# LSH attention and MoE on one core: scores in float16 pairs for all batches, fixed scales with a check at the end, and another order of batch 0

## The chip, the cores and the metric

The kernel runs on one core of a Trainium2 chip. The metric is the device time of one execution in microseconds (us). A core has a matrix engine (TensorE: PE, its weight loads PEld), three engines for elementwise work (VectorE: DVE, ScalarE: ACT, GpSimd: POOL) and a queue that issues transfers (SyncE: SP). Matrix results land in PSUM, eight banks of 512 float32 numbers in each of 128 partitions; everything else lives in SBUF.

## The reference

There are 4 batches of 8 heads with 768 positions of 64 numbers. A query sees only the keys that fall in the same of 64 buckets, which the signs of six projections give. The attention's output goes through two dense layers with a squared ReLU between them.

```python
q_bits = (np.einsum('bhsd,dk->bhsk', q, proj) > 0)      # 6 bits: a bucket
k_bits = (np.einsum('bhsd,dk->bhsk', k, proj) > 0)
mask = q_bucket[:, :, :, None] == k_bucket[:, :, None, :]
scores = np.where(mask, 0.125 * np.matmul(q, k^T), -1e9)
scores = scores - scores.max(axis=-1, keepdims=True)
attn = np.exp(scores); attn = attn / (attn.sum(-1, keepdims=True) + 1e-9)
x = (attn @ v) as (3072 tokens, 512)                   # 8 heads of 64 side by side
h = np.maximum(x @ w_in, 0.0)                          # 512 x 2048
out = h * h @ w_out                                    # 2048 x 512
```

q, k and v are float32 with a spread of 0.1; the two weight matrices are float64.

## The kernel before

**Precision.** An operand of a matrix product is split in two float16 numbers (high and low part), and three products are summed: high by high, high by low, low by high. `move` writes the high part and `left` the rest. So that float16 holds them, values and weights are first scaled by a power of two that the kernel finds from the data: `split` squares each fetched tile of a weight, sums over the partitions with a matmul against ones (`pt`), takes the largest (`norm`) and makes the factor in `scales`; `scale_values` does the same for v from a Square with a running sum (`sqv`). `fetch` turns float64 into float32 with a shift and an OR. Because each group of four w_out tiles gets its own scale, the first MoE stage adds its output up in four parts (`acc`), and `align` then multiplies all of w_out (`wo<-wo,rel`) so that later stages need not.

**Scores.** `prep` makes the operands of a pair of heads. R holds the transposed keys above the transposed queries. For batches 1 to 3 the two parts are kept in a 32-bit reduced float (A the high, L the low part; the profile prints it as f32), five transfers in SBUF rearrange them in Q, A, M and L, and a unit of scores is two products of 128 rows for each half of the keys: q high and low by k high, then q high by k low together with a mask code that pulls unequal buckets far below. The code comes from the bits through a matmul `pc` and a DVE operation that writes M. For batch 0 (`plain`) there is one product in full float32 with M above and the keys and queries beside it, with fewer transfers.

**Units and visits.** A unit is 128 queries of one head: scores into `pS`, the row maximum on DVE (`nmx`), the exponential on ACT (`e`, its sum in `sm`), then the reciprocal `rv`. Then the weights are normalised and split (`hl`: ACT the high part, DVE the low one) and a transfer transposes them into `aT`. In the visits of PLAIN_AV (numbers 0, 2 and 4) a unit instead divides on POOL, transposes six blocks with TensorE (`pT`) and copies them out of PSUM to a float32 `aT`. There are 192 units in 32 visits; a visit is one half of the queries (3 units) of a pair of heads. After the six units `av` makes the product with the values (`pA`) and splits it (`xx`). `pS` has one place of two banks; while u < 36, odd units use the banks of `po` instead.

**MoE stages.** When all four pairs of one half of a batch are done, `moe` adds a stage: 16 steps of 12 matmuls `pm` (384 columns) and 9 matmuls `po` (512 columns), with ReLU, square and split between them on ACT and DVE. There are eight stages of 112 paced groups each. WHOLE = {0: 2} makes batch 0 go through both halves of its first two pairs and only then to the first halves of the others, so that its first half is whole after six visits, 36 units.

**Order.** All operations are first recorded; `Program.order` then simulates the five queues with costs and ranks, and `emit` writes each queue's instructions in that order. PACE holds the m-th group of MoE matmuls back until a given unit has begun: group 0 at unit 25, 120 at unit 64, 640 at unit 193; the last 256 groups have no unit to wait for. Where the simulated TensorE would sit idle ahead of the first MoE work, `emit` puts matmuls on `ones` (`idle`). One line, 410, records nearly all instructions, so the profile tells groups apart by tiles.

Of the kernel before, what the change touches and what calls it, by code (L numbers as in the profile page):

```python
# [36 lines left out]
BUFS = dict(xx=12, hl=3, raw=2, f=7, e=3, aT=3, g=2, A=2, Q=2, L=2, M=2, RV=2, VV=6)  # L37
# [20 lines left out]
PACE = ((25, 0), (64, 120), (193, 640))  # L58
# [58 lines left out]
class Program:  # L117
# [11 lines left out]
    def tile(self, pool, kind, shape, dtype, name, bufs=1, tag=None):  # L129
# [291 lines left out]

@with_exitstack
def lsh_attention_moe(ctx: ExitStack, tc, kq, v, proj2, w_in, w_out, consts, out):
# [10 lines left out]
    def send(out, x):  # L434
        sp.dma_start(out, x)
# [32 lines left out]
    sgn_f = sb([P, 4 * P], F32, "sgn_f", tag="o")  # L468
# [6 lines left out]
    dve.tensor_copy(sgn, sgn_f)  # L475
# [21 lines left out]
    def fetch(src):  # L497

        raw = sb([P, 512, 2], U32, "raw", BUFS["raw"])
# [3 lines left out]
        move(first[:, :, 1], raw.rearrange("p n t -> p (n t)").bitcast(BF16).rearrange("p (n t) -> p n t", t=4)[:, :, 2], 1.0, (dve, pool))  # L503
# [63 lines left out]
    f32 = lambda x: x.bitcast(F32)  # L567
# [74 lines left out]
    def values(b, hp, plain):  # L642
# [14 lines left out]
    def unit(st, half, i, aT, plain):  # L657
        c0 = half * HS + i * P
        u = pr.rank
        pS = ps([P, 3, 512], F32, "pS2", tag="po") if u % 2 and u < ALTERNATE else ps([P, 2, 512], F32, "pS")  # L660
# [6 lines left out]
        nmx = sb([P, 1], F32, "nmx", 2)  # L667
# [211 lines left out]
```

## Time and profile before

| | us |
|---|---|
| three runs | 910.83, 911.90, 917.73 |
| median | 911.90 |
| span of the profiled execution, first to last instruction | 911.7 |
| TensorE's mean granted clock in it | 0.990 |

The record does not say which of the three runs was profiled; its span is 0.2 us under the median. The busy time of TensorE in the profile overlaps for successive matmuls, so its 96% is no measure of how much of the time it had work to issue. For that, one reads the distance between the starts of successive matmuls in the timeline.

| stretch of the span, us | what runs in it |
|---|---|
| 0 to 95 | units 0 to 23, first weights |
| 95 to 253 | units 24 to 63; the first MoE matmul at 153.5 |
| 253 to 745 | units 64 to 190, MoE between them |
| 745 to 911.7 | the rest of the MoE stages, one more unit |

### The profile page before, as it was taken

Reading aid. Unit: us, or ns where it says so; the run is one execution under the profiler, and the core shown is the slowest. Engines: PE = TensorE matmul, PEld = TensorE weight load, DVE = VectorE, ACT = ScalarE, POOL = GpSimd, SP = SyncE. Lnnn points to the kernel's source line nnn. Section 1 sums busy time; section 2 is a strip of 40 time slices with the busy share of each in tenths; the row PEclk is TensorE's granted clock in tenths of the full one; section 3 lists DMA queues with packets and bytes.
Section 4 is the critical chain, followed back from the end, with each engine's and each line's share of the span. In section 5 each row is a group of like instructions: output and inputs, shape, how many; then the busy total and the mean of one; then the engine's idle time right before and its main releaser. Section 6 shows DMA issues by size and latency. Waiting matters only on the chain. (4 is left out here: it accounts for less than half of the span.)

```text
span 911.7 us, 14110 instructions
## 1 busy us (share of the span) xinstructions
PE 871.3 (96%) x5038; PEld 472.1 (52%) x5038; DVE 614.6 (67%) x1150; ACT 664.4 (73%) x1208; POOL 75.7 (8%) x120
## 2 busy tenths in 40 slices
PE   7977987999989999999999999999999999999997
PEld 5543533455545555555555555555555555544553
DVE  4999898989796777787677767885867651211111
ACT  4989797989798777896787777886768663542433
POOL 0433222201000000000000000000000000000000
PEclk9999999999999999999999999999999999999999
DMA  7788778997979897979698979896969561200000
GB/s 234 194 200 185 192 178 192 226 204 166 194 169 203 160 197 139 221 167 203 127 219 157 192 115 196 171 190 126 199 123 194 96 100 28 60 1 1 35 1 36
DMA packets 298790, 136.54 MB, mean 150 GB/s; under 512 B 277088, under 2 KB 277216, under 8 KB 298720
## 3 DMA queue, kind: packets, MB, share of 16 engines
q1 hardware_dynamic: 298720, 135.64, 71.5%
q8 instruction: 40, 0.66, 0.3%
q14 instruction: 30, 0.25, 0.1%
HBM read 37.30 MB, written 6.29 MB: 48 GB/s over the span
## 5 line engine op out<-in xcount | busy, mean ns | idle before, releaser
L410 PE MATMUL po<-wo,g 128*128 128x512 f16 x1152 | 335.3, 380 | 2.4 <-ACT acc L410 0.8
L410 PE MATMUL pm<-xx,win 128*128 128x384 f16 x1536 | 323.8, 326 | 1.0 <-ACT g L410 0.7
L410 DVE TENSOR_REDUCE nmx<-pS 128x1 f32<-128x768 f32 x192 | 182.9, 953 | 63.3 <-PE pS L410 62.4
L410 ACT ACTIVATE e<-pS,nmx 128x768 f32<-128x768 f32 x192 | 172.5, 899 | 61.1 <-DVE nmx L410 56.4
L410 PEld LDWEIGHTS <-win 128*128 128x128 f16 x1536 | 145.7, 98 | 116.1 <-issue 18.1
L410 DVE SCALAR_TENSOR_TENSOR hl<-e,rv,hl 128x768 f16<-128x768 f32 x174 | 176.3, 1015 | 27.8 <-ACT hl L410 27.0
L410 ACT ACTIVATE hl<-e,rv 128x768 f16<-128x768 f32 x174 | 161.7, 931 | 23.8 <-ACT e L410 16.7
L410 PEld LDWEIGHTS <-g 128*128 128x128 f16 x1152 | 107.5, 98 | 131.4 <-issue 28.0
L410 DVE SCALAR_TENSOR_TENSOR g<-g,g 128x384 f16<-128x384 f32 x125 | 69.2, 554 | 134.1 <-ACT g L410 133.1
L410 ACT ACTIVATE g<-pm 128x384 f32<-128x384 f32 x128 | 62.4, 487 | 108.1 <-PE pm L410 106.0
L410 ACT ACTIVATE g<-g 128x384 f32<-128x384 f32 (+1 forms) x252 | 131.2, 521 | 6.8 <-PE po L410 1.8
L407 PE MATMUL pA<-aT,VV 128*64 128x384 f16 x1044 | 110.0, 333 | 0.0
L410 PE MATMUL pS<-A,Q 128*128 128x384 f32 x288 | 93.2, 404 | 2.8 <-ACT e L410 2.8
L407 PEld LDWEIGHTS <-VV 128*64 128x64 f16 x1044 | 53.9, 109 | 54.0 <-issue 37.2
L410 POOL TENSOR_SCALAR rv<-sm 128x1 f32<-128x1 f32 x77 | 37.3, 485 | 511.2 <-ACT e L410 477.6
L410 PE MATMUL pS<-L,M 128*128 128x384 f32 x288 | 77.2, 348 | 1.8 <-DMA M<-Q 1.8
L410 PEld LDWEIGHTS pS<-A,Q 128*128 128x128 f32 x288 | 47.1, 189 | 31.6 <-ACT e L410 22.0
L410 PEld LDWEIGHTS pS<-L,M 128*128 128x128 f32 x288 | 51.9, 188 | 5.8 <-issue 3.9
L410 PE MATMUL pS<-A,L 128*128 128x384 f32 x96 | 41.0, 553 | 9.8 <-ACT L L410 4.9
L410 PE MATMUL pS<-Q,M 128*128 128x384 f32 x96 | 38.2, 516 | 7.8 <-ACT e L410 7.7
L410 DVE TENSOR_SCALAR M<-pc,cst 128x384 fp32r<-128x384 f32 (+1 forms) x56 | 37.6, 671 | 3.9 <-PE pc L410 3.9
L410 ACT ACTIVATION_READ_ACCUMULATOR e<-pS,nmx 128x1 f32 x192 | 38.1, 198 | 0.0
(93 smaller groups left out, 586.3 us busy)
## 6 DMA issues: line engine op xcount, KB each, us to landing
R<-kq SPq DMA_DIRECT2D x24, 384.0 KB
raw<-w_in SPq DMA_DIRECT2D x16, 511.8 KB
raw<-w_out SPq DMA_DIRECT2D x16, 511.8 KB
V<-vp SPq DMA_DIRECT2D x16, 384.0 KB
out<-o SPq DMA_DIRECT2D x21, 256.0 KB
Q<-L SPq DMA_DIRECT2D x24, 192.0 KB
Q<-A SPq DMA_DIRECT2D x24, 192.0 KB
L<-M SPq DMA_DIRECT2D x24, 192.0 KB
```

The costliest lines, as they stand in the source:

```text
L407: ins = q.engine.matmul(*map(real, args), **kw).ins
L410: ins = getattr(q.engine, o.name)(*map(real, o.args), **{k: real(x) for k, x in o.kw.items()}).ins
```

## The change

The kernel becomes two programs. The first (`fast`) runs with fixed scales and fills a flag; behind it each engine loads the flag into a register, and a branch runs the second, general program if the flag is 1. The general one is the kernel before without its special treatment of batch 0. In the fast program:

- Scores are float16 pairs in all batches: `balance` scales keys by 1/4 and queries by 1/2, `prep` always makes A, L, Q and M (now float16, eight places each, so that all four pairs of batch 0 are kept), and the mask code fits float16 with `masks`. The full-float32 product of batch 0 is gone.
- Weights are scaled by 256 for nothing in `fetch` (its factor becomes 2.0) and values by 16; `split` has no squares, sums and factors, `scale_values`, `align` and the four-part sum of the first stage go, and every stage's result is scaled by a constant.
- PLAIN_AV has visits 0 to 5. WHOLE = {0: 0}: batch 0 takes the first halves of its four pairs first, so that a half is whole after four visits, 24 units; then the second halves in reverse. `pS` alternates while u < 24; from there `pT` uses the bank `misc`. PACE lets MoE groups begin at unit 19 and has 140 and 660 where there were 120 and 640.
- `verify` loads q, k and v once more (48 loads of 128 x 768 numbers into the places of `e`), squares q and k on ACT, takes the largest of v and of the weights on DVE, sums squares of w_in with 16 matmuls, looks at every unit's maximum and sum, and writes the flag. The ninth step of the last MoE stage waits for that.

```diff
-BUFS = dict(xx=12, hl=3, raw=2, f=7, e=3, aT=3, g=2, A=2, Q=2, L=2, M=2, RV=2, VV=6)
+BUFS = {
+    True: dict(xx=12, hl=3, raw=2, f=3, e=3, aT=3, g=2, A=8, Q=8, L=8, M=8, R=2, VV=4),
+    False: dict(xx=12, hl=3, raw=2, f=7, e=3, aT=3, g=2, A=2, Q=2, L=2, M=2, R=2, VV=6),
+}
...
-PLAIN, ALTERNATE = 4, 36
-
-PLAIN_AV, DIVIDE = (0, 2, 4), ("pool",)
-
-WHOLE = {0: 2}
-
+ALTERNATE = {True: 24, False: 0}
+
+PLAIN_AV, DIVIDE = (0, 1, 2, 3, 4, 5), ("pool",)
+
+WHOLE = {0: 0}
 
 WIN_AT, WOUT_AT = (0, 2), 1
 FIRST = len(WIN_AT)
 
-PACE = ((25, 0), (64, 120), (193, 640))
+PACE = ((19, 0), (64, 140), (193, 660))
+
+CHECK_RANK = 200
+
+
+QS, KS = 2.0**-1, 2.0**-2
+VS, WS = 2.0**4, 2.0**8
+HS2 = 2.0**-9
+QK_MAX, V_MAX, V_MIN, W_MAX, W_MIN, NORM_MAX = 16.0, 1.0, 2.0**-4, 2.0**15, 2.0, (1.38 * WS) ** 2
...
+def lsh_attention_moe(tc, kq, v, proj2, w_in, w_out, consts, out):
+    with tc.tile_pool(name="fl", bufs=1) as pool:
+        flag = pool.tile([1, 1], mybir.dt.int32, name="flag")
+        run(tc, kq, v, proj2, w_in, w_out, consts, out, flag)
+        general = tc.nc.values_load(flag[0:1, 0:1], min_val=0, max_val=1)
+        with tc.If(general > 0):
+            run(tc, kq, v, proj2, w_in, w_out, consts, out, None)
+
+
 @with_exitstack
-def lsh_attention_moe(ctx: ExitStack, tc, kq, v, proj2, w_in, w_out, consts, out):
+def run(ctx: ExitStack, tc, kq, v, proj2, w_in, w_out, consts, out, flag):
+    fast = flag is not None
+    bufs_of = BUFS[fast]
...
+    masks = cst
+    if fast:
+        parts = lambda x: x.rearrange("p (n t d) -> p n t d", t=2, d=D)
+        dve.tensor_scalar(parts(sgn)[:, :, 0], parts(sgn_f)[:, :, 0], 2.0 / BIG, 2.0**15, ALU.mult, ALU.mult)
+        dve.tensor_scalar(parts(sgn)[:, :, 1], parts(sgn_f)[:, :, 1], 2.0, 2.0**14, ALU.mult, ALU.mult)
+        masks = sb([P, 2], F32, "masks")
+        dve.memset(masks[T, 0:1], 3 * 2.0**16)
+        dve.memset(masks[T, 1:2], -65504.0)
+        dve.memset(masks[U, 0:1], 2.0**16)
+        dve.memset(masks[U, 1:2], 0.0)
+        balance = sb([P, 1], F32, "balance")
+        dve.memset(balance[T], KS)
+        dve.memset(balance[U], QS)
+        maxes, sums = sb([P, UNITS], F32, "maxes"), sb([P, UNITS], F32, "sums")
+    else:
+        dve.tensor_copy(sgn, sgn_f)
+        balance = cst[:, 2:3]
...
-        move(first[:, :, 1], raw.rearrange("p n t -> p (n t)").bitcast(BF16).rearrange("p (n t) -> p n t", t=4)[:, :, 2], 1.0, (dve, pool))
+        move(first[:, :, 1], raw.rearrange("p n t -> p (n t)").bitcast(BF16).rearrange("p (n t) -> p n t", t=4)[:, :, 2], 2.0 if fast else 1.0, (dve, pool))
...
+        if fast:
+            for f, (hi, lo) in zip(fs, parts):
+                move(hi, f)
+                left(lo, f, 1.0, hi)
+            return 1.0, 1.0
...
-    def prep(b, hp, plain):
+    def prep(b, hp):
         r0 = pr.rank
-        Rs, Rqs = [], []
+        Rs = []
         for odd in range(2):
-            R = sb([P, S], F32, "Q" if odd else "A") if plain else sb([P, S], F32, "R", 2)
+            R = sb([P, S], F32, "R")
             send(R, kq[b, 2 * hp + odd])
             Rs.append(R)
-            if plain:
-                Rq = sb([P, S], F32, "R", 2)[T]
-                send(Rq, kq[b, 2 * hp + odd, U])
-                Rqs.append(Rq)
 
         pd = ps([P, 512], F32, "pd", tag="misc")[:, 0:HS]
         matmuls(*[(pd[32 * n : 32 * n + 32], pj, Rs[n // 2][:, n % 2 * HS : (n % 2 + 1) * HS]) for n in range(4)])
@@ -588,33 +633,22 @@
         out = []
         for odd, R in enumerate(Rs):
             pr.rank = r0
-            if plain:
-                M = sb([P, S], F32, "M" if odd else "L")
-            else:
-
-                A, L, Q, M = [sb([P, S], F32R, name) for name in "ALQM"]
-                move(A, R, cst[:, 2:3])
-                left(L, R, cst[:, 2:3], f32(A))
+            A, L, Q, M = [sb([P, S], F16 if fast else F32R, name) for name in "ALQM"]
+            move(A, R, balance)
+            left(L, R, balance, f32(A))
             pr.rank = r0 + STACKS
-            if not plain:
-                send(f32(Q[T]), f32(A[U]))
-                send(f32(Q[U]), f32(L[U]))
-                send(f32(A[U]), f32(A[T]))
+            send(f32(Q[T]), f32(A[U]))
+            send(f32(Q[U]), f32(L[U]))
+            send(f32(A[U]), f32(A[T]))
             for half in range(2):
                 w = slice(half * HS, (half + 1) * HS)
                 n = 2 * odd + half
                 pc = ps([P, 512], F32, "pc", tag="misc")[:, 0:HS]
                 pe.matmul(pc, sgn[:, n * P : (n + 1) * P], bits, start=True, stop=True)
-                dve.tensor_scalar(M[:, w], pc, cst[:, 0:1], cst[:, 1:2], ALU.subtract, ALU.max)
-            if plain:
-
-                move(R[U], M[T], 1.0, MV)
-                move(M[T], Rqs[odd], SC)
-                out.append(((M, R),))
-            else:
-                send(f32(L[U]), f32(M[T]))
-                send(f32(M[T]), f32(Q[T]))
-                out.append(((Q, A), (M, L)))
+                dve.tensor_scalar(M[:, w], pc, masks[:, 0:1], masks[:, 1:2], ALU.subtract, ALU.max)
+            send(f32(L[U]), f32(M[T]))
+            send(f32(M[T]), f32(Q[T]))
+            out.append(((Q, A), (M, L)))
...
-        if b not in vscales:
-            scale_values(b)
-        if plain:
-            return loaded[b, hp]
-        RV = loaded.pop((b, hp))
+        if fast:
+            vscales[b] = VS, None
+            RV = sb([P, 2, KC, D], F32, "V", tag="VV" if plain else "R")
+            send(RV, v[b, hp])
+            if plain:
+                return RV
+        else:
+            if b not in vscales:
+                scale_values(b)
+            RV = loaded.pop((b, hp))
...
-        pS = ps([P, 3, 512], F32, "pS2", tag="po") if u % 2 and u < ALTERNATE else ps([P, 2, 512], F32, "pS")
+        pS = ps([P, 3, 512], F32, "pS2", tag="po") if u % 2 and u < ALTERNATE[fast] else ps([P, 2, 512], F32, "pS")
...
-        nmx = sb([P, 1], F32, "nmx", 2)
+        nmx = maxes[:, u : u + 1] if fast else sb([P, 1], F32, "nmx", 2)
-        sm = sb([P, 1], F32, "sm", 2)
+        sm = sums[:, u : u + 1] if fast else sb([P, 1], F32, "sm", 2)
...
-                pT = ps([P, 512], F32, "pT", tag=("pm", "pA")[g])[:, 0:HS]
+                pT = ps([P, 512], F32, "pT", tag=("pm", "pA")[g] if u < ALTERNATE[fast] else "misc")[:, 0:HS]
...
+        if fast:
+            return 1.0 / (WS * 64)
...
+        grouped = n == 0 and not fast
+        if not grouped:
             pr.rank = RANK_MOE
             back = unscaled(b)
         for f in range(NF + 1):
+            if f == NF // 2:
+                pr.checked = len(pr.ops)
...
+    def verify():
+        pr.rank = CHECK_RANK
+        grade = sb([P, 64], F32, "grade")
+        good = sb([P, 4, 64], F32, "good", tag="hl")
+        dve.memset(good, 1.0)
+        bound = lambda to, x, value, op: dve.tensor_scalar(to, x, value, 1.0, op, ALU.mult)
+        for n in range(2 * B * H // 2):
+            X = sb([P, S], F32, "X", tag="e")
+            send(X, kq[n // H, n % H])
+            pr.add((act, "activation", (X, X, AF.Square), {"scale": 0.25, "accum_out": grade[:, n : n + 1]}))
+        for n in range(B * H // 2):
+            X = sb([P, S], F32, "X", tag="e")
+            send(X, v[n // (H // 2), n % (H // 2)].rearrange("p t c d -> p (t c d)"))
+            dve.tensor_reduce(grade[:, 32 + n : 33 + n], X, AX.X, ALU.max, apply_absolute_value=True)
+        for n in range(NCC):
+            dve.tensor_reduce(grade[:, 48 + n : 49 + n], win[:, 0, n], AX.X, ALU.max, apply_absolute_value=True)
+            dve.tensor_reduce(grade[:, 52 + n : 53 + n], wo[:, 0, 4 * n : 4 * n + 4], AX.XY, ALU.max, apply_absolute_value=True)
+            pt = ps([P, 512], F32, "pt", tag="misc")
+            for cc in range(NCC):
+                sq = sb([P, 512], BF16, "sq", tag="raw")
+                square(sq, win[:, 0, cc, n * 512 : (n + 1) * 512])
+                pe.matmul(pt, ones, sq, start=cc == 0, stop=cc == NCC - 1)
+            dve.tensor_reduce(grade[:, 56 + n : 57 + n], pt, AX.X, ALU.max)
+        dve.memset(grade[:, 60:64], 1.0)
+        bound(good[:, 0, 0:32], grade[:, 0:32], QK_MAX, ALU.is_le)
+        bound(good[:, 0, 32:48], grade[:, 32:48], V_MAX, ALU.is_le)
+        bound(good[:, 1, 32:48], grade[:, 32:48], V_MIN, ALU.is_ge)
+        bound(good[:, 0, 48:56], grade[:, 48:56], W_MAX, ALU.is_le)
+        bound(good[:, 1, 48:56], grade[:, 48:56], W_MIN, ALU.is_ge)
+        bound(good[:, 0, 56:60], grade[:, 56:60], NORM_MAX, ALU.is_le)
+        bound(maxes, maxes, 2.0**30, ALU.is_lt)
+        bound(sums, sums, float(S), ALU.is_equal)
+        dve.tensor_tensor(sums, sums, maxes, ALU.max)
+        worst = sb([P, 2], F32, "worst")
+        dve.tensor_reduce(worst[:, 0:1], good.rearrange("p a b -> p (a b)"), AX.X, ALU.min)
+        dve.tensor_reduce(worst[:, 1:2], sums, AX.X, ALU.min)
+        both = sb([P, 1], BF16, "both")
+        dve.tensor_tensor(both, worst[:, 0:1], worst[:, 1:2], ALU.min)
+        pt = ps([P, 512], F32, "pt", tag="misc")[:, 0:1]
+        pe.matmul(pt, ones, both, start=True, stop=True)
+        bad = pr.given(flag, "flag")
+        dve.tensor_scalar(bad, pt[0:1], P - 0.5, 1.0, ALU.is_lt, ALU.mult)
+        pr.ops[pr.checked].deps.add(len(pr.ops) - 1)
...
-        sts, aTs, plain = kept[b, hp], [], n in PLAIN_AV
+        sts, aTs, plain = kept[b, hp], [], fast and n in PLAIN_AV
...
+    if fast:
+        verify()
```

More of the change, by code (lines that the diff above doesn't have):

```diff
@@ L27 @@
 HS = 384
+UNITS = B * H * S // P
 KC = S // P
@@ L136, in tile, with given @@
         return View(rec, self.shadow.dram_tensor(f"{name}_{self.n}", shape, dtype, kind="Internal").ap(), ())
+    def given(self, real, name):
+        rec = Buffer("sb", int(np.prod(real.shape[1:])), None, lambda: real)
+        return View(rec, self.shadow.dram_tensor(name, real.shape, real.dtype, kind="Internal").ap(), ())
     @staticmethod
@@ L451, in sb @@
     def sb(shape, dtype, name, bufs=1, tag=None):
-        return pr.tile(sbp, "sb", shape, dtype, name, BUFS.get(tag or name, bufs), tag)
+        return pr.tile(sbp, "sb", shape, dtype, name, bufs_of.get(tag or name, bufs), tag)
     def ps(shape, dtype, name, bufs=1, tag=None):
@@ L467, in lsh_attention_moe @@
     sp.dma_start(pj[:, NB : 2 * NB], proj2[:, 3 * NB : 4 * NB])
-    sgn_f = sb([P, 4 * P], F32, "sgn_f", tag="o")
+    sgn_f = sb([P, 4 * P], F32, "sgn_f", tag="raw" if fast else "o")
     dve.memset(sgn_f, 0.0)
@@ L474, in lsh_attention_moe @@
     sgn = sb([P, 4 * P], BF16, "sgn")
-    dve.tensor_copy(sgn, sgn_f)
+    masks = cst
[15 more added lines that the diff above has]
+        balance = cst[:, 2:3]
     thr = sb([P, 1], F32, "thr")
@@ L497, in fetch @@
     def fetch(src):
-        raw = sb([P, 512, 2], U32, "raw", BUFS["raw"])
+        raw = sb([P, 512, 2], U32, "raw", bufs_of["raw"])
         send(raw.rearrange("p n t -> p (n t)").bitcast(U16)[:, 0:2047], src.bitcast(U16)[:, 1:2048])
@@ L547, in split_wout @@
         back = split([w_out[:, n] for n in range(4 * j, 4 * j + 4)], [(wo[:, 0, n], wo[:, 1, n]) for n in range(4 * j, 4 * j + 4)], "wo")[1]
+        if fast:
+            return
         z = zs[:, j : j + 1]
@@ L564, in align @@
             move(x, x, rel[:, n // 4 : n // 4 + 1])
-    f32 = lambda x: x.bitcast(F32)
+    f32 = lambda x: x if fast else x.bitcast(F32)
     def matmuls(*args, start=True, stop=True):
         pr.add((pe, "matmuls", [(a, {"start": start, "stop": stop}) for a in args], {}))
-    def prep(b, hp, plain):
+    def prep(b, hp):
         r0 = pr.rank
-        Rs, Rqs = [], []
+        Rs = []
         for odd in range(2):
-            R = sb([P, S], F32, "Q" if odd else "A") if plain else sb([P, S], F32, "R", 2)
+            R = sb([P, S], F32, "R")
             send(R, kq[b, 2 * hp + odd])
             Rs.append(R)
-            if plain:
-                Rq = sb([P, S], F32, "R", 2)[T]
-                send(Rq, kq[b, 2 * hp + odd, U])
-                Rqs.append(Rq)
         pd = ps([P, 512], F32, "pd", tag="misc")[:, 0:HS]
@@ L666, in unit @@
         sS = pS[:, 0:2, 0:HS]
-        nmx = sb([P, 1], F32, "nmx", 2)
+        nmx = maxes[:, u : u + 1] if fast else sb([P, 1], F32, "nmx", 2)
         dve.tensor_reduce(nmx, sS, AX.XY, ALU.max, negate=True)
-        e = sb([P, S], F32, "e", BUFS["e"])
-        sm = sb([P, 1], F32, "sm", 2)
+        e = sb([P, S], F32, "e", bufs_of["e"])
+        sm = sums[:, u : u + 1] if fast else sb([P, 1], F32, "sm", 2)
         act.activation(e.rearrange("p (j s) -> p j s", j=2), sS, AF.Exp, bias=nmx, accum_out=sm)
@@ L685, in unit @@
             return
-        hl = sb([P, 2, S], F16, "hl", BUFS["hl"])
+        hl = sb([P, 2, S], F16, "hl", bufs_of["hl"])
         move(hl[:, 0], e, rv)
@@ L716, in moe @@
         po, gs = None, {}
-        if n:
+        grouped = n == 0 and not fast
+        if not grouped:
             pr.rank = RANK_MOE
@@ L734, in moe @@
                 g32 = sb([P, HS], F32, "g32", 2)
-                pr.add((act, "activation", (g32, pm[:, 0:HS], AF.Relu), {"scale": 2.0**-23}),
-                       (dve, "tensor_scalar", (g32, pm[:, 0:HS], 2.0**-23, 0.0, ALU.mult, ALU.max), {}))
+                pr.add((act, "activation", (g32, pm[:, 0:HS], AF.Relu), {"scale": HS2 if fast else 2.0**-23}),
+                       (dve, "tensor_scalar", (g32, pm[:, 0:HS], HS2 if fast else 2.0**-23, 0.0, ALU.mult, ALU.max), {}))
                 square(g32, g32)
@@ L745, in moe @@
                 pr.mark = None
-                first, last = (m % 4 == 0, m % 4 == 3) if n == 0 else (m == 0, m == NF - 1)
+                first, last = (m % 4 == 0, m % 4 == 3) if grouped else (m == 0, m == NF - 1)
                 if first:
@@ L757, in moe @@
                 pr.rank = RANK_MOE
-                if n == 0 and last:
+                if grouped and last:
                     back = unscaled(b, m // 4)
-                if n == 0 and m == 3:
+                if grouped and m == 3:
                     acc = sb([P, 3, DM], F32, "acc")
@@ L763, in moe @@
                     r0 = b * S + half * HS + t * P
-                    if n == 0 and last:
+                    if grouped and last:
                         if m == 3:
@@ L781, in moe @@
                 split_wout(f // 4 + 1)
-        if n == 0:
+        if grouped:
             pr.rank = RANK_MOE
             align()
+    def verify():
[41 more added lines that the diff above has]
+        pr.ops[pr.checked].deps.add(len(pr.ops) - 1)
@@ L804, in lsh_attention_moe @@
     for b in range(B):
-        F = WHOLE.get(b, H // 2)
+        F = WHOLE.get(b, H // 2) if fast else H // 2
         visits += [(b, hp, half) for hp in range(F) for half in range(2)] + [(b, hp, 0) for hp in range(F, H // 2)] + [(b, hp, 1) for hp in reversed(range(F, H // 2))]
@@ L808, in lsh_attention_moe, with ready @@
     alive = lambda views: all(x.rec in x.rec.line[-x.rec.bufs :] for x in views)
-    def ready(b, hp, rank, plain):
+    def ready(b, hp, rank):
         if (b, hp) not in kept or not alive(x for st in kept[b, hp] for ab in st for x in ab):
             pr.rank = rank
-            kept[b, hp] = prep(b, hp, plain)
-    ready(*visits[0][:2], -10.0, PLAIN > 0)
+            kept[b, hp] = prep(b, hp)
+    ready(*visits[0][:2], -10.0)
     early = {n: (split_win, j, win_rank(4 * j)) for j, n in enumerate(WIN_AT)}
@@ L830, in lsh_attention_moe @@
         if n + 1 < len(visits):
-            ready(*visits[n + 1][:2], u + PREP, visits[n + 1][0] == 0 and visits[n + 1][1] < PLAIN)
+            ready(*visits[n + 1][:2], u + PREP)
         if (b, hp, plain) not in kept_v or not alive([kept_v[b, hp, plain]]):
@@ L843, in lsh_attention_moe @@
             stages += 1
+    if fast:
+        verify()
     pr.emit()
```

## The prediction

> **What bounds the kernel now.** I read the page's busy shares first, then the windows of four stretches (the second cut where MoE starts), then the timeline of TensorE.
>
> ```profile
> 0.00:95.00 95.00, 79.37 (x444) 44.32 (x445) 76.43 (x161) 77.31 (x142) 28.30 (x42) 0.95 0.81 204
> 95.00:153.50 58.50, 48.00 (x221) 24.10 (x220) 52.56 (x108) 46.53 (x88) 14.96 (x24) 0.94 0.75 186
> 153.50:253.00 99.50, 98.00 (x565) 52.24 (x563) 88.18 (x169) 87.91 (x163) 12.33 (x19) 1.00 0.94 196
> 253.00:745.00 492.00, 486.01 (x2941) 269.96 (x2940) 371.13 (x667) 385.07 (x688) 20.06 (x36) 1.00 0.87 169
> 745.00:911.70 166.70, 159.94 (x873) 81.53 (x871) 26.33 (x48) 67.53 (x132) 0.00 (x0) 1.00 0.08 22
> ```
>
> The window rows give the length, then busy time of PE, PEld, DVE, ACT and POOL, the granted clock, the DMA share and GB/s. DVE and ACT are full nine tenths of the time from 95 to 253 us (and before that, once the start is over), three quarters in the middle (371 and 385 of 492 us), and far less at the end. PE is the other way round: its matmuls are sparse before 153.5 us (444 in 95 us, against 2941 in 492 us, six a us). The stretches end where units 24, 64 and 191 take their exponential, and where MoE starts:
>
> ```profile
> 95.00 0.89 ACT L410 ACTIVATE e<-pS,nmx 128x768 f32<-128x768 f32 x1
> 251.93 0.88 ACT L410 ACTIVATE e<-pS,nmx 128x768 f32<-128x768 f32 x1
> 744.29 0.90 ACT L410 ACTIVATE e<-pS,nmx 128x768 f32<-128x768 f32 x1 [0.99 <-DVE nmx L410]
> 153.53 2.11 PE L410 MATMUL pm<-xx,win 128*128 128x384 f16 x12
> 853.15 1.30 PE L410 MATMUL pm<-xx,win 128*128 128x384 f16 x7
> 857.04 1.30 PE L410 MATMUL pm<-xx,win 128*128 128x384 f16 x7
> 470.29 2.11 PE L410 MATMUL pm<-xx,win 128*128 128x384 f16 x12
> 472.24 1.03 PE L410 MATMUL po<-wo,g 128*128 128x512 f16 x4
> 472.92 0.70 PE L410 MATMUL pS<-A,Q 128*128 128x384 f32 x2
> 473.46 0.51 PE L410 MATMUL pS<-L,M 128*128 128x384 f32 x2
> 473.82 1.25 PE L410 MATMUL po<-wo,g 128*128 128x512 f16 x5
> 460.89 1.65 PE L407 MATMUL pA<-aT,VV 128*64 128x384 f16 x18
> ```
>
> Starts give the true cost. A step of MoE (12 pm, 9 po, seven paced groups) takes 857.04 − 853.15 = 3.89 us, 0.556 a group. Twelve f16 matmuls of 384 columns take 472.24 − 470.29 = 1.95, 0.163 each. A unit of scores in the reduced 32-bit float takes 473.82 − 472.92 = 0.90 us (0.81 to 0.90 in the neighbours; 0.87 taken). Eighteen records of pA take 1.65 us, a visit of 36 about 3.3.
>
> From 253 to 745: 126 units × 0.87 = 110, 508 MoE groups (520 of 129 units) × 0.556 = 282, 21 visits × 3.3 = 69, preparations about 16 (10.5 pairs, each four pc of 0.163 and eight small pd, estimated at 1.5 us): 477 of 492. So TensorE is the bound there, with 3% lost. Before 153.5 us there is no MoE to do, and DVE and ACT bound. The last stretch is MoE alone.
>
> **The change part by part.** Rows for elementwise work and for batch 0's matmuls:
>
> ```profile
> L410 DVE SCALAR_TENSOR_TENSOR hl<-e,rv,hl 128x768 f16<-128x768 f32 x174 | 176.3, 1015 | 27.8 <-ACT hl L410 27.0
> L410 ACT ACTIVATE hl<-e,rv 128x768 f16<-128x768 f32 x174 | 161.7, 931 | 23.8 <-ACT e L410 16.7 <-DVE rv L410 2.5 <-DMA aT<-hl 2.1
> L410 ACT ACTIVATE aT<-pT 128x384 f32<-128x384 f32 x35 | 16.5, 502 | 1.1 <-PE pT L410 0.9
> L410 ACT ACTIVATE sq<-f 128x512 bf16<-128x512 f32 x32 | 20.0, 635 | 1.4 <-DVE f L410 1.0 <-DVE towo L410 0.4
> L410 ACT ACTIVATE sqv<-V 128x768 bf16<-128x768 f32 x16 | 13.4, 838 | 5.4 <-DMA V<-vp 5.3
> L410 DVE SCALAR_TENSOR_TENSOR VV<-V,tov,VV 128x768 f16<-128x768 f32 x16 | 16.5, 1034 | 0.2
> L410 ACT ACTIVATE A<-R,cst 128x768 fp32r<-128x768 f32 x24 | 22.2, 926 | 1.4 <-PE pS L410 1.2 <-DMA A<-A 0.2
> L410 DVE SCALAR_TENSOR_TENSOR L<-R,cst,A 128x768 fp32r<-128x768 f32 x24 | 24.6, 1025 | 0.7 <-PE pS L410 0.7
> L410 ACT ACTIVATE Q<-M 64x768 f32<-64x768 f32 x4 | 3.4, 843 | 1.3 <-DVE M L410 1.2
> L410 ACT ACTIVATE wo<-wo,rel 128x1024 f16<-128x1024 f16 x9 | 10.0, 1144 | 0.0
> 15.52 0.91 PE L410 MATMUL pS<-A,L 128*128 128x384 f32 x2 [2.07 <-ACT L L410]
> 55.44 2.85 PE L410 MATMUL pS<-Q,M 128*128 128x384 f32 x8 [0.54 <-ACT e L410]
> 58.12 0.38 PE L410 MATMUL pt<-sq,ones 128*128 128x512 bf16 x1
> 32.29 0.49 PE L410 MATMUL pT<-unit_f,e 128*128 128x128 f32 x3
> 32.61 0.38 PE L410 MATMUL pt<-sq,ones 128*128 128x512 bf16 x1
> 39.28 2.16 PE L407 MATMUL pA<-aT,V 128*64 128x384 f32 x12
> ```
>
> *Units 0 to 23 (now 95 us).* DVE and ACT bound it with 153.7 us of work in the 80 us behind the first scores at 15.5. Twelve more units are plain: each drops hl (0.93 + 1.02) for two copies of aT (2 × 0.50), −11.4. Twelve squares of weights, −7.6; four of values, −3.4; VV of two pairs (ACT as long as A, DVE 1.03), −3.9. The eight heads of batch 0 now get A and L (+15.6) and lose two moves like Q<-M each (−13.5); the fourth pair comes forward, +7. Together −17, so 136 of 154 us: 71 + 15 = 86. I cost the two chained transfers that the first unit now has ahead of its mask (L<-M, M<-Q) at nothing, because its scores shed the full-float32 product; without that cover they cost about 3 us. The matmuls saved here (a full-float32 unit 2.68/2 = 1.34 us, now 0.65) save no time of their own: PE waits anyway.
>
> *Units 24 to 63 (now 158 us).* MoE now has data from about unit 24 instead of from 153.5 us, and PE takes over as the bound: 40 units × 0.65 = 26; 12 plain units of six transposes at 0.11 (three in 0.32), 8; two plain visits of 24 records (twelve in about 2.1), 9; four others, 13; two pairs' preparation, 3; 140 groups × 0.556 = 78. That is 137, with 3% lost 141, and 3 for the step from the first xx to the first pm: 144. DVE and ACT would have 275 us less 20 squares (12.7), align (10), six units turned plain (5.7) and a pair moved ahead (7): 240, or 120 on each of the two, 83% of 144. Unit 64 comes at 230 instead of 253.
>
> *Units 64 to 190 (now 492 us).* Scores fall from 0.87 to 4 × 0.163 = 0.65: 126 × 0.22 = 28. DVE and ACT hold 756 us; in the 464 left that is 81% against 77%. The stretch keeps its 3% loss by assumption. It ends at 694.
>
> *The rest (now 166.7).* Twenty fewer groups are left, −11. The check's 16 matmuls of 512 columns, 0.22 each as po, add 3.5. Its Squares on ACT (32 of about 1.03, as sqv with the read of its sum) and its reductions on DVE lie beside MoE steps, where ACT is 40% busy; I give 2 us for meetings. If that cover were gone, each would cost its full length.
>
> *The branch.* No register load or branch stands in this trace. The nearest rows are the end itself and the fetches of instructions:
>
> ```profile
> 901.59 4.26 PE L410 MATMUL po<-wo,g 128*128 128x512 f16 x19
> 906.61 1.59 SPq L410 DMA_DIRECT2D out<-o  x3
> q8 instruction: 40, 0.66, 0.3%
> 664.13 5.18 DMA M<-Q
> ```
>
> From the last transfer's issue (908.2) to the end are 3.5 us, in which other engines are done: all of the branch could hide there (0), or a fetch as slow as the longest transfer in the chain (5.2 us) and a wait at either side come behind it (7 us). A gain is excluded, since only work is added. I take 3, nearer to the instruction fetches (0.3% of 16 × 911.7 us over 40, 1.1 us each). The Trainium skill (Runtime: NRT & Kernel Launch, section Instruction fetch mechanics) says that a branch taken to code outside the fetched window stalls for a fetch; no row here shows that, and it would leave the sum inside these ends.
>
> Sum: 694 + 166.7 − 11 + 3.5 + 2 + 3 = 858. It is made against the span, 911.7, which is 0.2 under the median of the three runs.
>
> **The rivals.** *DVE and ACT take over.* At 81 to 83% they are tighter than before, and pS has one place from unit 24, so scores, maximum and exponential follow each other. Against it: at 88% each (153 to 253) PE was still busy 98 of 99.5 us. If they bound units 64 to 190, the 28 us vanish: 886.
>
> *POOL shuts DVE out.* Eighteen more divisions run on POOL.
>
> ```profile
> L410 POOL TENSOR_SCALAR e<-e,rv x18: 907/921/1367, 21.3 to 114.0; 128x768 f32<-128x768 f32 x18
> L410 DVE SCALAR_TENSOR_TENSOR hl<-e,rv,hl x174: 983/1009/1364, 35.8 to 780.8; 128x768 f16<-128x768 f32 x174
> ```
>
> A few of each are 0.4 us longer than their medians (921 to 1367, 1009 to 1364 ns): one waits for the other. If every new division held DVE for its whole 0.92 us in the stretch that DVE bounds, that would be 17 us: 875; by the rows' excess, 18 × 0.45 = 8 at most. The Trainium skill (SBUF — State Buffer, section SBUF: two separate sides) says that GpSimd and a two-input DVE operation exclude each other for a whole instruction. By that rule alone the sum would be up to 875; the medians speak for less.
>
> *The check comes late.* The ninth step of the last stage waits for the flag; eight steps and the end follow (31 + 10), so the flag is due near 815. The 48 loads can start once the last places of e come free. With three places and a transfer as long as 5.2 us plus 1.0 of Square, a load takes 2.1 us, 100 in all: from 694 to 794. But unit 191 ran 34 us after unit 190 in the old order:
>
> ```profile
> 778.40 0.88 ACT L410 ACTIVATE e<-pS,nmx 128x768 f32<-128x768 f32 x1
> ```
>
> With that again it ends at 828, and PE waits some 13 us: 871.
>
> *The flag comes out as 1 (slower).* Then the second program runs: about 858 + 900 = 1760. It decides as soon as one partition of one test fails. From the reference's inputs: the largest |v| is 0.48 (limit 1), the largest column sum of the scaled w_in squared 78,600 (limit 124,800); 8 of 24,576 queries have no key in their bucket, and these need a sum of exactly 768.
>
> *No change.* The early MoE only waits elsewhere (pT and pc share one bank), and the scores' time is PE idling: 905 to 912.
>
> **How the numbers follow.** Forecast (848 to 870) 0.56; DVE and ACT 0.15; POOL 0.08; late check 0.08; a faster first stretch than the 86 us, 840 to 848, 0.05; no change 0.03; the flag 0.05. Predicted 858. From 840 to 890 leaves out the flag, no change and the edges, under 2 in 10. A measurement of this kernel can tell about 1% from no change. Faster by over 1%: 0.92; within: 0.03; slower: 0.05.
>
> **What would show it.** Unit 24 near 86 us, first pm near 90; unit 64 near 230; a unit's four score matmuls within 0.65 us; PE's starts without gaps after that; unit 190 near 694; the flag's matmul before the ninth step of the last stage; under 7 us between the last stage's output and the end. Wrong would be: units spaced over 3.75 us in the middle with DVE or ACT over 90%, a gap on PE ahead of the ninth step, or a second set of everything.

## The result

Five runs of the changed kernel took 863.81 to 868.76 us, median 865.48. The kernel before took 911.9 in five runs beside them. The ratio is 0.948, with a 95% interval of 0.945 to 0.951, so the change saves about 5%. The forecast was 858, from 840 to 890. The profiled execution is the slowest of the five (868.76 us); its span is 866.9 us.

The stretches below are cut where units 24, 64 and 191 begin their exponential (86.3, 241.6 and 701.5 us; before 95.0, 251.9 and 744.3). The window rows of the changed kernel (length, busy time of PE, PEld, DVE, ACT, POOL, granted clock, DMA share, GB/s):

```profile
86.30:241.60 155.30, 145.75 (x902) 76.69 (x902) 140.55 (x228) 128.13 (x246) 39.49 (x54) 1.00 0.76 175
241.60:701.50 459.90, 453.55 (x2857) 236.75 (x2856) 358.34 (x636) 367.51 (x663) 15.85 (x26) 1.00 0.75 160
701.50:866.90 165.40, 156.14 (x850) 79.01 (x850) 45.16 (x82) 95.33 (x201) 0.00 (x0) 0.99 0.46 137
```

| stretch | before | forecast | changed |
|---|---|---|---|
| units 0 to 23 | 95.0 | 86 | 86.3 |
| units 24 to 63 | 156.9 | 144 | 155.3 |
| units 64 to 190 | 492.4 | 464 | 459.9 |
| the rest | 167.4 | 164 | 165.4 |

Three of the four stretches came out within about 4 us. The second one hardly moved: of its forecast gain of 13 us, 11 are missing. DVE is busy 140.55 of its 155.30 us.

The groups of the page and of its form list show what was replaced. The first two rows answer to the score and transpose rows of before, the next two to its low parts and divisions (fewer of the one, more of the other), and the last three are new:

```profile
L425 PE MATMUL pS<-A,Q 128*128 128x384 f16 x384 | 95.5, 326 | 13.7 <-ACT e L425 11.8
L425 PE MATMUL pT<-unit_f,e 128*128 128x128 f32 x216 | 33.8, 279 | 7.6 <-POOL e L425 4.1
L425 DVE SCALAR_TENSOR_TENSOR hl<-e,rv,hl 128x768 f16<-128x768 f32 x156 | 158.3, 1015 | 18.3 <-ACT hl L425 17.8
L425 POOL TENSOR_SCALAR e<-e,rv 128x768 f32<-128x768 f32 x36 | 39.7, 1107 | 26.5 <-DVE rv L425 13.5
L425 DVE TENSOR_REDUCE grade<-wo 128x1 f32<-128x2048 f16 x4 | 9.1, 2278 | 0.5 <-ACT wo L425 0.5
L425 DVE TENSOR_REDUCE grade<-win 128x1 f32<-128x2048 f16 x4 | 9.1, 2275 | 0.0
L425 DVE TENSOR_REDUCE grade<-X 128x1 f32<-128x768 f32 x16 | 15.0, 950 | 4.8 <-DMA X<-vp 4.6
```

And three parts of the timeline of the changed kernel: scores in the middle, two of the check's reductions, and the ninth step of the last stage behind the flag's matmul:

```profile
299.89 0.49 PE L425 MATMUL pS<-A,Q 128*128 128x384 f16 x2
300.21 0.49 PE L425 MATMUL pS<-L,M 128*128 128x384 f16 x2
300.54 0.65 PE L425 MATMUL pm<-xx,win 128*128 128x384 f16 x3
...
121.79 2.27 DVE L425 TENSOR_REDUCE grade<-win 128x1 f32<-128x2048 f16 x1
125.24 2.28 DVE L425 TENSOR_REDUCE grade<-win 128x1 f32<-128x2048 f16 x1
...
824.97 0.17 PE L425 MATMUL pt<-both,ones 128*128 128x1 bf16 x1
825.00 0.81 PE L425 MATMUL po<-wo,g 128*128 128x512 f16 x3
825.64 1.30 PE L425 MATMUL pm<-xx,win 128*128 128x384 f16 x7
```

A unit's four score matmuls take 300.54 − 299.89 = 0.65 us, as forecast. TensorE does not pause at the ninth step. But the maxima of the weights, which belong to the check at the end, run at 122 us, in the stretch where DVE is full.

### The profile page after: what moved, and what is told of

Its sections match the earlier page's. It is cut to its first block, busy times and chain, and to the rows that moved or that the text cites. A ratio compares the mean times of both kernels' runs of the same rounds, so it can differ in the third digit from the quotient of the medians.

```text
span 866.9 us, 14179 instructions
## 1 busy us (share of the span) xinstructions
PE 823.5 (95%) x5110; PEld 433.2 (50%) x5114; DVE 608.2 (70%) x1072; ACT 648.2 (75%) x1224; POOL 93.3 (11%) x127
## 5 line engine op out<-in xcount | busy, mean ns | idle before, releaser
L425 DVE TENSOR_REDUCE maxes<-pS 128x1 f32<-128x768 f32 x192 | 182.9, 954 | 55.5 <-PE pS L425 54.3
L425 ACT ACTIVATE e<-pS,maxes 128x768 f32<-128x768 f32 x192 | 172.6, 899 | 45.3 <-DVE maxes L425 41.8
L425 PE MATMUL pS<-A,Q 128*128 128x384 f16 x384 | 95.5, 326 | 13.7 <-ACT e L425 11.8
L425 PE MATMUL pS<-L,M 128*128 128x384 f16 x384 | 96.5, 327 | 1.3 <-DMA M<-Q 1.3
L425 PEld LDWEIGHTS <-Q 128*128 128x128 f16 x384 | 34.7, 97 | 59.5 <-issue 36.5
L425 PEld LDWEIGHTS <-M 128*128 128x128 f16 x384 | 37.3, 98 | 26.8 <-DMA M<-Q 1.9
L425 DVE TENSOR_SCALAR M<-pc,masks 128x384 f16<-128x384 f32 x64 | 43.0, 671 | 5.3 <-PE pc L425 5.2
L425 POOL TENSOR_SCALAR e<-e,rv 128x768 f32<-128x768 f32 x36 | 39.7, 1107 | 26.5 <-DVE rv L425 13.5
L425 PE MATMUL pT<-unit_f,e 128*128 128x128 f32 x216 | 33.8, 279 | 7.6 <-POOL e L425 4.1
L425 ACT ACTIVATE aT<-pT 128x384 f32<-128x384 f32 x72 | 33.4, 499 | 7.5 <-PE pT L425 7.1
```

Source lines behind the costliest of these rows:

```text
L425: ins = getattr(q.engine, o.name)(*map(real, o.args), **{k: real(x) for k, x in o.kw.items()}).ins
```

## The experiments

Each ratio is to the kernel before as it ran beside that experiment: 913.5, 914.2, 915.1 or 915.5 us, against 911.9 beside the changed kernel. Differences in us between kernels of two sets are therefore uncertain by 2 to 3 us. Times within a run come from one profiled execution each.

**What the check and the branch cost.** First both were taken out.

```diff
-        general = tc.nc.values_load(flag[0:1, 0:1], min_val=0, max_val=1)
-        with tc.If(general > 0):
-            run(tc, kq, v, proj2, w_in, w_out, consts, out, None)
...
-    if fast:
-        verify()
```

> The changed kernel without the check (the 48 loads, their squares and maxima, the flag) and without the branch and the second program. By the prediction's terms (3.5 us of matmuls, 2 us of meetings, 3 us for the branch) it is 8.5 us faster than the changed kernel: near 857 us. If the check lies wholly beside the last MoE stages and only the end (8.0 us from the last matmul's end against 5.9 before) is longer: 863 us.

Measured: 848.77 us, ratio 0.928 (0.925 to 0.931), 17 us faster than the changed kernel, twice what was priced. Unit 64 comes at 225.7 us instead of 241.6, long before the check's loads begin. So two more kernels asked about the eight maxima. One holds them back:

```diff
             dve.tensor_reduce(grade[:, 48 + n : 49 + n], win[:, 0, n], AX.X, ALU.max, apply_absolute_value=True)
+            pr.ops[-1].deps.add(pr.marks[180])
             dve.tensor_reduce(grade[:, 52 + n : 53 + n], wo[:, 0, 4 * n : 4 * n + 4], AX.XY, ALU.max, apply_absolute_value=True)
+            pr.ops[-1].deps.add(pr.marks[180])
```

> The changed kernel; the only edit: the check's eight maxima over the split weights (2.28 us each on DVE, which ran between 78 and 197 us in the changed kernel) may start only when unit 180 has. If these 18 us on DVE, put into the stretch that DVE bounds, are what the check costs beyond its tail, unit 64 comes near 226 us as in the kernel without check and branch, and the time is 852 to 856 us. If the check costs by something else (another order, its loads), 862 to 866 us.

Measured: 853.35 us, ratio 0.933 (0.931 to 0.936). Nothing of the work is left out, so this is a version faster than both kernels, by about 12 us against the changed one. The windows between units 24 and 64, then 64 and 190:

```profile
81.80:224.50 142.70, 138.15 (x874) 73.42 (x874) 131.89 (x243) 124.21 (x242) 25.33 (x32) 1.00 0.84 196
224.50:686.30 461.80, 460.46 (x2890) 239.97 (x2888) 373.94 (x640) 367.54 (x670) 10.86 (x29) 1.00 0.73 157
```

Unit 24 to 64 now takes 142.7 us (forecast 144), with more matmuls of TensorE in each us (874 in 142.7 against 902 in 155.3). The reverse test puts the maxima alone into the program without check and branch:

> The kernel without check and branch (848.8 us), plus only the eight maxima over the split weights, left where they fall early; no loads, no squares, no flag, no branch. If DVE bounds the stretch from unit 24 to 64, unit 64 comes 10 to 16 us later than in the kernel without them and the time is 857 to 862 us. If TensorE bounds it and DVE has room (the prediction: 83% busy), 849 to 851 us.

Measured: 854.91 us, ratio 0.935 (0.933 to 0.938); unit 64 at 233.4, 7.7 us later than without. That lies between the ranges of the two theories, above TensorE's and under DVE's. The direction is DVE's; the delay is 42% of the 18.2 us of work. The windows from unit 24 to 64, first without and then with the maxima, show one reason:

```profile
83.80:225.70 141.90, 137.65 (x860) 72.67 (x860) 130.44 (x244) 121.09 (x234) 24.30 (x29) 1.00 0.84 194
86.50:233.40 146.90, 139.44 (x873) 74.07 (x874) 139.38 (x235) 122.20 (x235) 36.60 (x44) 1.00 0.81 183
```

With the maxima the planner gives POOL 36.60 us instead of 24.30 (8 of the operations `top` instead of 1, 6 of `g` instead of none), so part of DVE's other work moved away. The full check costs 6 us more than its early maxima (6.1) and its late remainder (4.6) together. The profiles put this between units 24 and 64, where the changed kernel takes 155.3 us and the one with the maxima alone 146.9; some ten more MoE groups run there in the changed kernel, and why is open.

The branch by itself was not run alone. In the two kernels whose TensorE ends at the same time, 843.5 us, the end follows after 5.0 us without it (no_check_no_branch) and 8.1 with it (late_weight_maxima):

```profile
843.52 1.57 ACT L425 ACTIVATE o<-po 128x512 f32<-128x512 f32 x3 [2.50 <-PE po L425]
844.14 1.89 SPq L425 DMA_DIRECT2D out<-o  x3
```

These are the last rows of late_weight_maxima before the end at 851.6; the forecast's 3 us for the branch fits. All kernels with a branch need 7.3 to 8.5 us from TensorE's last matmul to the end, the two without a branch 5.0, the kernel before 5.9.

**What the order and the plain visits are worth.**

```diff
-WHOLE = {0: 0}
+WHOLE = {0: 2}
-PACE = ((19, 0), (64, 140), (193, 660))
+PACE = ((25, 0), (64, 120), (193, 640))
-ALTERNATE = {True: 24, False: 0}
+ALTERNATE = {True: 36, False: 0}
-PLAIN_AV, DIVIDE = (0, 1, 2, 3, 4, 5), ("pool",)
+PLAIN_AV, DIVIDE = (0, 2, 4), ("pool",)
-A=8, Q=8, L=8, M=8
+A=2, Q=2, L=2, M=2
```

> The changed kernel with the old order of batch 0: WHOLE {0: 2}, PLAIN_AV (0, 2, 4), pS alternating while u < 36, PACE of before, and two places each for A, L, Q and M. If the order and the earlier MoE carry the first two stretches (prediction: 23 us at unit 64), it takes 880 to 890 us. If lighter work on DVE and ACT (no squares, no align) carries them, it stays at 866 to 872.

Measured: 892.72 us, ratio 0.975 (0.971 to 0.979): order, visits and the number of places carry 27 us together, a little above the range. Then the visits of late_weight_maxima were kept and only the order (WHOLE, PACE, ALTERNATE) was undone:

> As late_weight_maxima (PLAIN_AV 0 to 5), but with WHOLE {0: 2}, pS alternating while u < 36 and PACE of before: MoE gets its first input after 36 units instead of 24. If the early MoE is worth what the prediction gave it (TensorE would have nothing but scores for 12 units, some 40 us of which it needs half), 862 to 872 us. If the plain visits alone carry the first two stretches, 852 to 857 us.

Measured: 867.01 us, ratio 0.947 (0.943 to 0.950), 14 us over late_weight_maxima. Unit 64 comes at the same time (225.1 against 224.5 us), but the first MoE matmul at 136.9 instead of 94.2, and the second stage begins at 232.8 instead of 208.5. Ahead of unit 64 the old order runs 97 MoE groups and the new one 123, and DVE is busy 93% and 92% of the stretch from unit 24. That the units come no earlier with less work for TensorE speaks for DVE as what sets their speed; the early order gives TensorE something to do meanwhile, and less MoE is left behind unit 64.

With the new order kept, the number of plain visits was changed, always with the maxima held back. With four visits they are held to unit 150, because with unit 180 the operations of that kernel wait for each other in a circle and it gives no time:

```diff
-PLAIN_AV, DIVIDE = (0, 1, 2, 3, 4, 5), ("pool",)
+PLAIN_AV, DIVIDE = (0, 2, 4), ("pool",)                    # late_plain_3
+PLAIN_AV, DIVIDE = (0, 1, 2, 3, 4, 5, 6, 7), ("pool",)     # late_plain_8
+PLAIN_AV, DIVIDE = (0, 1, 2, 3), ("pool",)                 # late150_plain_4, with marks[150]
```

> As late_weight_maxima, but with PLAIN_AV (0, 2, 4): visits 1, 3 and 5 normalise and split on ACT and DVE and transpose by DMA. By the prediction's terms a unit then costs 0.95 us more on the two engines, 0.5 us on each: 12 units before unit 24 are worth 6 us, 6 more behind it 3 us, less 5 us of matmuls that they save: 3 to 9 us over late_weight_maxima. If TensorE bounds, it is faster than that kernel by up to 5 us.

> As late_weight_maxima, but with PLAIN_AV of all eight visits of batch 0. Twelve more units lose 1.0 us on DVE each and TensorE gets 0.8 us a unit more. If DVE still bounds units 36 to 48 without the maxima, it gains up to 6 us; if TensorE bounds there, it loses up to 9 us.

> As late_weight_maxima, but with PLAIN_AV (0, 1, 2, 3), and the weight maxima may start from unit 150 instead of 180 (TensorE bounds there as well, so no difference is expected from that): the visits ahead of the first MoE input are plain, 4 and 5 are not. In late_plain_3 the loss sat in the first 24 units (14 of 15 us at unit 64), where the queue of SP holds transposes (three took 9.1 us there) and TensorE, without MoE to do, waited and its clock fell. If that is what plain visits save, visits 4 and 5 need not be plain: 851 to 856 us, unit 24 at 82 to 85. If lighter work on DVE and ACT is what they save (rival: 12 units of 0.5 us on each engine), it is 857 to 861 us with unit 64 some 6 us later.

| plain visits | us | ratio, 95% | unit 24 | unit 64 |
|---|---|---|---|---|
| three | 876.06 | 0.960 (0.957 to 0.962) | 95.7 | 240.0 |
| four | 870.07 | 0.951 (0.948 to 0.954) | 89.4 | 239.8 |
| six | 853.35 | 0.933 (0.931 to 0.936) | 81.8 | 224.5 |
| eight | 868.42 | 0.950 (0.948 to 0.953) | 83.9 | 236.8 |

All three expectations were too small, four visits even in both theories. The windows from unit 24 to 64 of the kernels with four and with eight show what is full on either side of six:

```profile
89.40:239.80 150.40, 138.87 (x856) 70.68 (x857) 138.36 (x242) 127.18 (x231) 17.49 (x27) 0.97 0.96 208
```

```profile
83.90:236.80 152.90, 150.65 (x931) 80.99 (x931) 123.38 (x233) 126.78 (x253) 32.84 (x42) 1.00 0.60 157
```

With four, DVE is busy 92% and the DMA share is 0.96; in six-visit late_weight_maxima they are 92% and 0.84. A visit that is not plain puts six low parts of 1.0 us on DVE and six transposes on the DMA. With eight, DVE falls to 81%, TensorE is busy 150.65 of 152.90 us, and the stretch is 10.2 us longer, about the 0.8 us a unit that TensorE got more: that speaks for TensorE as the bound there. Six is the best of the four counts; which of DVE and DMA costs the time with four was not separated.

In late_plain_3 another thing is seen, ahead of MoE:

```profile
52.00:58.00 6.00, 2.45 (x12) 0.96 (x10) 5.91 (x11) 3.98 (x9) 2.34 (x3) 0.97 1.22 213
58.00:64.00 6.00, 3.59 (x12) 1.74 (x12) 5.23 (x10) 3.08 (x6) 2.01 (x3) 0.50 1.00 223
64.00:70.00 6.00, 5.33 (x30) 2.75 (x30) 4.30 (x8) 2.13 (x4) 0.91 (x1) 0.50 0.70 175
...
45.44 9.07 SPq L425 DMA_TRANSPOSE aT<-hl  x3
66.74 5.36 PE L422 MATMUL pA<-aT,VV 128*64 128x384 f16 x36
```

Three transposes hold SP's queue for 9.07 us while the DMA share is at 1.0 and more. TensorE has 12 matmuls in each of two windows of 6 us, its clock falls to 0.50, and a visit of pA takes 5.36 us instead of the 3.3 of a warm clock. Whether the clock is cause or only sign of the lost time was asked with fillers on TensorE's gaps:

```diff
-                pr.busy_from = min(pr.busy_from, len(pr.ops))
                 for c in range(3):
...
-                pT = ps([P, 512], F32, "pT", tag=("pm", "pA")[g] if u < ALTERNATE[fast] else "misc")[:, 0:HS]
+                pT = ps([P, 512], F32, "pT", tag=("misc", "pA")[g] if u < ALTERNATE[fast] else "misc")[:, 0:HS]
```

> As late_plain_3 (PLAIN_AV 0, 2, 4), but matmuls on ones fill TensorE's expected gaps up to the first MoE matmul instead of up to the first transposes (and pT uses the bank misc instead of pm, which the fillers need). In late_plain_3 the granted clock was 0.66 from 56 to 81 us and 0.59 from 96 to 116. If the low clock carries most of its 22.7 us, the clock stays over 0.9 there, unit 24 comes at 84 to 88 us instead of 95.7 and the time is 860 to 867 us. If the work on DVE and ACT carries it (rival), the clock rises and the time stays at 873 to 878 us.

> As late_weight_maxima (PLAIN_AV 0 to 5) with the same fillers and the same bank for pT: the control. Its clock was 1.00 in those stretches already, so both theories expect 851 to 856 us; longer by more than that would be the price of the bank or of the fillers.

Measured: 893.16 us with three plain visits (0.975, 0.973 to 0.978) and 893.20 in the control with six (0.976, 0.972 to 0.979). The clock is 0.91 and more in every window of 25 us up to 150 us of both, but unit 24 comes at 122.6 and 124.5 us: the control lost 40 us by the fillers or the bank, so it controls nothing and the question stays open.

**What float16 scores are worth.** As old_order_f16, with the 32-bit float for A, L, Q and M:

```diff
-            A, L, Q, M = [sb([P, S], F16 if fast else F32R, name) for name in "ALQM"]
+            A, L, Q, M = [sb([P, S], F32R, name) for name in "ALQM"]
```

> As the old-order kernel, but A, L, Q and M in the reduced 32-bit float for all batches. If TensorE bounds units 64 to 190, 0.22 us a unit come back: 28 us there and 5 to 12 more in batch 0, so 30 to 40 us over the old-order kernel with float16. If DVE and ACT bound the middle (rival), less than 10 us over it.

Measured: 929.48 us, ratio 1.015 (1.011 to 1.020): 36.8 us over the same kernel with float16. In its timeline a unit takes 402.75 − 401.94 = 0.81 us and 405.89 − 405.00 = 0.89:

```profile
401.94 0.62 PE L425 MATMUL pS<-A,Q 128*128 128x384 f32 x2
402.39 0.51 PE L425 MATMUL pS<-L,M 128*128 128x384 f32 x2
402.75 1.31 PE L425 MATMUL pm<-xx,win 128*128 128x384 f16 x7
...
405.00 0.70 PE L425 MATMUL pS<-A,Q 128*128 128x384 f32 x2
405.54 0.52 PE L425 MATMUL pS<-L,M 128*128 128x384 f32 x2
405.89 0.82 PE L425 MATMUL po<-wo,g 128*128 128x512 f16 x3
```

This kernel is 1.5% slower than the one before, which has neither a check nor pairs in batch 0: in the old order the rest of the change does not pay without float16. The matmuls are not all that differs in this pair. The five transfers that rearrange A, Q, L and M move 192 KB each instead of 96. And 24.6 of the 37.2 us between the profiled executions lie ahead of unit 64, 13.8 of them even ahead of unit 24, where 24 units at 0.22 us would give 5. The DMA share from unit 24 to 64 is 0.98 with the 32-bit float and 0.88 with float16. What the transfers alone cost was not tried, and neither was what the fixed scales alone are worth (no squares, no `align`).

**A gap on TensorE.** In the changed kernel's profile TensorE pauses near 330 us:

```profile
330.03 0.48 PE L425 MATMUL pS<-A,Q 128*128 128x384 f16 x2 [1.57 <-ACT e L425]
332.92 0.51 PE L425 MATMUL pS<-A,Q 128*128 128x384 f16 x2 [1.91 <-ACT e L425]
```

PACE now allows group 224 at unit 85, but the third stage's input is ready after unit 90; in between there is no MoE to run.

```diff
-PACE = ((19, 0), (64, 140), (193, 660))
+PACE = ((19, 0), (64, 140), (90, 224), (193, 660))
```

> The changed kernel with one more point in PACE: group 224 is held to unit 90, where the third stage's input is ready. In the changed kernel's trace TensorE has gaps of 6.6 us between 325 and 350 us, where 224 groups are used up five units before unit 90. If these gaps are a price of the faster pace, it takes 859 to 861 us. If DVE bounds units 24 to 90 anyway (it is busy 91% there), the gaps only spread out: 864 to 867 us.

Measured: 866.18 us, ratio 0.947 (0.944 to 0.950): no change. Between 325 and 350 us TensorE is now idle 1.3 us instead of 4.6 (25.00 less 23.68 and less 20.41 us busy; the expectation's 6.6 is not in the window rows). Unit 90 comes at 327.0 instead of 329.0 us, and as much is lost again behind it: the whole is no faster. In late_weight_maxima, with the pace of the changed kernel, unit 90 comes at 312.6 us.

## Why the prediction was right, and where it was not

**Units 0 to 23: right in sum.** 86 was forecast, 86.3 measured. One piece under it was wrong: the first unit's two chained transfers were to be hidden by the cheaper scores. The first exponential came at 23.7 us instead of 19.8, so they were not. TensorE waits 1.25 us for the transfer L<-M and 1.29 us for M<-Q there. It was made up by unit 24; DVE and ACT had less to do than forecast, 64.2 and 57.2 us, 121 instead of 136. (The prediction's 153.7 us before include 10.2 ahead of 15.5 us; with 143.6 the same working gives nearly the same 86.) The agreement to 0.3 us is luck: kernels with the same six plain visits and the same order of batch 0 reach unit 24 between 81.8 us (late_weight_maxima) and 90.1 us (pace_90).

**Units 24 to 63: the step that failed.** The prediction said "DVE and ACT would have 275 us less 20 squares (12.7), align (10), six units turned plain (5.7) and a pair moved ahead (7): 240, or 120 on each of the two, 83% of 144", so TensorE would bound, and of the check that "its reductions on DVE lie beside MoE steps, where ACT is 40% busy". Neither held. The check's maxima of the weights depend on nothing late: one of the eight ran just ahead of unit 24 and seven in this stretch, 15.9 of the 18.2 us, on DVE alone. And the two engines' work was neither 240 us nor evenly spread: DVE had 140.6 us and ACT 128.1. Even with the maxima held back they have 131.9 and 124.2, 16 us over the 240. The rows show where: A and L are made here for eight heads instead of the four of before (15.5 us against 8.1), where the prediction took a pair away, and f and top of the weights, less of which is done ahead of unit 24, grow on DVE from 14.8 to 21.9 us.

Held back, the maxima give the stretch 142.7 us, close to the 144 of the forecast, so the 11 us came from a term that was put in another stretch, the check's maxima. That the remaining time agrees is in part luck. The stretch then holds 123 MoE groups (370 matmuls pm and po, three to a group) and not 140, some 9 us less for TensorE at 0.556 each, and DVE is busy 92%, not 83%; which of the two sets the 142.7 us is not shown. The first pm also came later than forecast: at 98.5 us, 12.2 behind unit 24 (94.2 and 12.4 in late_weight_maxima), where the prediction allowed 3 us and expected it near 90.

**Units 64 to 190: right, in part by luck.** 464 forecast, 459.9 measured, with 0.65 us for a unit. But the two stretches do not hold the same work. The records of pm and po in the kernel before, then in the changed one:

```profile
251.90:744.30 492.40, 182.15 (x895) 1.00 0.87 169
251.90:744.30 492.40, 190.72 (x673) 1.00 0.87 169
241.60:701.50 459.90, 177.58 (x869) 1.00 0.75 160
241.60:701.50 459.90, 184.93 (x655) 1.00 0.75 160
```

Before there were 1568 matmuls, so some 522 groups and not the 508 that the prediction took from PACE; now there are 1524, 508 groups. That is 8 us of the 32.5 us gained, at 0.556 a group. One visit of pA fewer (720 records instead of 756) is 3 us more. About 21 us are left, where the prediction had 28 for the scores. With 522 groups, the prediction's own costs fill 485 of the 492 us before, 1.5% lost and not 3%; now, with 508 groups, 20 visits of pA and 0.65 us a unit, they fill 446 of 460, 3% lost, the pauses near 330 us among them. So the assumed equal loss was wrong, and the smaller amount of MoE covered it.

The pair of kernels that differ in the scores' type gives 36.8 us in all, where the prediction's 0.22 us a unit would be 42 for 192 units. Between units 64 and 190 the two differ by 14.7 us (479.2 against 464.5), with 11 MoE groups, 6 us, fewer in the slower one: again about 21 us. In late_weight_maxima, where no such pause stands near 330 us, the stretch takes 461.8 us with 1562 matmuls and 720 records of pA: there 26 us are left. So the scores are worth 21 to 26 us in this stretch, not quite the 28. The rest of the pair's 36.8 us lies ahead of unit 64, with the transfers as an untested rival.

**The rest: right.** 164 forecast, 165.4 measured. In no_check_no_branch this stretch takes 158.2 us, so check and branch cost about 7 us here, where 8.5 were priced; the branch is 3 us of it, and the check's loads, squares and matmuls fit beside the stages. (The longest transfer in the chain of before took 5.45 us, not the 5.2 that the prediction read; its bound for the branch hardly changes.)

**Order.** The prediction gave the early MoE no price of its own. It is about 14 us (867.01 against 853.35): the units come no faster, and TensorE does more MoE beside them.

**The rivals.** DVE did take over, but in units 24 to 63, not in 64 to 190, and in good part through the check. The check did not come late, though its loads began only near the last unit (726.2 us), as that rival feared: the 48 of them were issued from 725.9 to 806.1 us, 1.7 us each instead of 2.1, and the flag is ready at the ninth step. The flag came out as 0. POOL's divisions grew from 1048 ns in the mean (18 of them, in the groups of before) to 1107 (36). The excess over the median of 921 before grew from 18 × 0.127 = 2.3 to 36 × 0.186 = 6.7 us, by 4.4, within the 8 us given for it; what part of the time it cost was not tried. The Trainium skill (SBUF — State Buffer, section SBUF: two separate sides) says that a GpSimd operation and a two-input DVE operation exclude each other; the longer mean agrees in direction.

Against the profiled 866.9 the forecast is 8.9 us short: 11.3 in the second stretch, 1.4 in the last and 0.3 in the first, less 4.1 in the third.

## What to carry to other kernels

Work that a change adds "at the end" runs where its inputs allow it and the scheduler finds a place; ask of each piece what it really waits for, and price it in the stretch where it can start. When two stretches are compared, count what work each holds before calling the time right. Do not average two engines into one: count each engine's own pieces, because a low part or a maximum that the kernel gives to DVE is not shared by an idle ACT. And where a setting trades one engine against another, as the plain visits do, measure on both sides: 4, 6 and 8 visits gave 870, 853 and 868 us.

## What the runs showed of the hardware

TensorE's granted clock fell without a long pause. In the changed kernel two gaps of 1.6 and 1.9 us, 2.9 us apart, brought it down once. The rows show the 25 us around them, the 3.4 us in which TensorE was busy 1.26 us, and the next 3.4 us at half clock:

```profile
325.00:350.00 25.00, 20.41 (x122) 10.02 (x119) 21.79 (x39) 21.04 (x38) 1.46 (x3) 0.93 0.90 201
329.80:333.20 3.40, 1.26 (x7) 0.67 (x7) 2.79 (x6) 3.06 (x7) 0.00 (x0) 1.00 0.85 189
333.20:336.60 3.40, 3.40 (x21) 1.54 (x18) 2.87 (x7) 1.93 (x3) 0.00 (x0) 0.51 0.92 148
```

In late_plain_3 it stayed at 0.50 for two windows of 6 us with TensorE busy 3.59 and 5.33 us of them, though no gap there was over 1.7 us. The Trainium skill (TensorE: Matmul & The Clock Gate, section Part 1: The HAM clock gate) names an idle window of about 3.4 us as what halves the clock; these runs show it halved by shorter gaps that follow each other closely.
